# Two-stage kernel (sparse attention, then spectral mixing): uneven weight pieces, a joint mix of last rows, overwritten matmul passes, and separate tiles for z and y

## The chip, the core and the metric

The kernel runs on one NeuronCore of a Trainium2 chip. The metric is the device time of the whole kernel in microseconds (us). The core has a matrix engine (TensorE, "PE" in the profile, with its weight loads "PEld"), a vector engine (VectorE, "DVE"), a scalar engine (ScalarE, "ACT"), GpSimd ("POOL"), a sync engine ("SP") and sixteen transfer engines (DMA). Weights and attention inputs are issued from GpSimd, because these transfers convert from float32 to float16 on the way. Outputs are issued from the sync engine.

## What is computed

The first stage is an attention over 8 batches, 8 heads, 576 tokens and 64 dimensions, with two masks (local for the first four heads, strided for the others). Its result `x` (8 x 576 x 512) goes through the second stage:

```python
X = np.fft.rfft(x, axis=1)
Y = np.zeros_like(X)
Xr, Xi = (np.real(X[:, :n_modes]), np.imag(X[:, :n_modes]))      # n_modes = 64
Yr = np.einsum('bmd,mde->bme', Xr, w_r) - np.einsum('bmd,mde->bme', Xi, w_i)
Yi = np.einsum('bmd,mde->bme', Xr, w_i) + np.einsum('bmd,mde->bme', Xi, w_r)
Y[:, :n_modes] = Yr + 1j * Yi
y = np.fft.irfft(Y, n=S, axis=1)
u = x + y
return (u + np.maximum(u @ w_ch, 0.0)).astype(np.float32)
```

The weights `w_r` and `w_i` hold 64 x 512 x 512 float32 numbers each, so the two together are 134 MB to be read; everything else is small beside them.

## The kernel before

The kernel splits the 512 input columns of each mode into two halves and so has 128 "half modes". They are loaded two at a time into one tile: 64 partitions for the real part, 64 for the imaginary part.

```python
ORDER = [(1, m) for m in range(SPLIT1)] + [(0, m) for m in range(SPLIT0)]
ORDER += [(1, m) for m in range(SPLIT1, NM)] + [(0, m) for m in range(SPLIT0, NM)]
# in w_fetch, for the pair that starts at place i of ORDER:
for ri, src in enumerate((moe_w_r, moe_w_i)):
    dst = wt[ds(64 * ri, 64)]
    ...                                   # rows: the same 64 rows of the source
    ones = range(2)
    if ri and not m:
        ones = [1]
    elif i < 2 * NM - 4:
        nc.gpsimd.dma_start(dst, rows)    # both modes of the pair in one transfer
        continue
    for j in ones:                        # the last four half modes: one transfer for each
        nc.gpsimd.dma_start(dst[:, j], rows[:, j])
```

Each half mode is multiplied in `mode` (16 passes of 128x128 against 16 columns, line 555). While these stream, the kernel turns `x` (`turn`), multiplies it by `w_ch` (`premix`, kept as `v0`, and `x` itself as `xo`), and, as soon as 16 modes are complete, computes their spectra `zz` (multiplied by `w_ch`) and `yy`:

```python
def spec_out(g, b, yp, zp):
    src, dst = ds(32 * (b % 4), 32), ds(32 * g, 32)
    act_copy(zzs[b][dst], zp[src])                              # ScalarE
    nc.vector.tensor_copy(out=yys[b][dst], in_=yp[src])         # VectorE, line 688

def spec_pair(g, bq):                     # the third group, g = 2
    up = psum("u", pair=True)
    zp, yp = up[:, 0], up[:, 1]
    spec_mm(g, bq, yp, zp)
    for b in range(4 * bq, 4 * bq + 4):
        spec_out(g, b, yp, zp)
```

Then `renew` adds the first 48 modes' share to `v0` and `xo`, two row groups at a time, or the last 64 rows of two batches together. One `renew` follows each of the last modes:

```python
def renew(b, ts):
    n = len(ts)
    ...
    vp, up = psum("v", pair=True), psum("u", pair=True)
    for j, t in enumerate(ts):
        nc.tensor.matmul(vp[:, j], idn, v0[:, j], start=True, stop=False)       # line 889
        rows_of(b, t, vp[:, j], zzs, False)                                     # line 696
    act_copy(v0, vp[:, 0:n])
    for j, t in enumerate(ts):
        rows_of(b, t, up[:, j], yys, True)
    nc.vector.tensor_tensor(out=xo, in0=up[:, 0:n], in1=xo, op=AluOp.add)       # line 894

rest = [(0, m) for m in range(SPLIT1, NM)] + [(1, m) for m in range(SPLIT0, NM)]   # 24 modes
NL = len(rest) - 2
for i, (slot, m) in enumerate(rest):
    mode(slot, m)
    upto = min(len(late), -(-len(late) * i // (NL - 1)))
    for w in late[n:upto]:                # 2 spec_pair, then 20 renew
        w()
    n = upto
    if i == NL - 1:
        v_early(0); u_early(0)            # lines 921 and 930: v0 and xo into the accumulators
    elif i == NL:
        u_early(1)
```

After the last mode the tail begins: the last 16 modes' `zp` and `yp` (lines 672 and 679), then for each output item its own rows (`v_early`, `u_early`), the new rows (line 941), a relu on ScalarE (line 955), a sum on VectorE (line 963) and the output transfer (line 971). An item is 128 rows of two batches, 512 KB of output; the last 64 rows of two batches make one of 256 KB.

The last 64 rows of each batch lie in the same tile `xT` as the others before, and `premix` handles them batch by batch with 64 output rows:

```python
xT, cols = xTs[b], out_cols(t)
if t < 4:
    pr = ds(0, 128)
    ...
else:
    pr = ds(64 * (b % 2), 64)
    v0, xo = v0h[b // 2], xoh[b // 2]
for ch in range(4):
    nc.tensor.matmul(vp[pr, :], xT[:, ch, cols], w_chs["cp"][:, ch, :], start=(ch == 0), stop=(ch == 3))
for ch in range(4):
    nc.tensor.transpose(tp[pr, ds(128 * ch, 128)], xT[:, ch, cols], idn)
```

Of the kernel before, what the change touches and what calls it, by code (L numbers as in the profile page):

```python
# [56 lines left out]
def kernel(  # L57
# [91 lines left out]
    ORDER = [(1, m) for m in range(SPLIT1)] + [(0, m) for m in range(SPLIT0)]  # L149
    ORDER += [(1, m) for m in range(SPLIT1, NM)] + [(0, m) for m in range(SPLIT0, NM)]  # L150
    w_tiles = []
    w_chs = {}
    w_ch = big.tile([128, 4, DM], F16, name="w_ch")

    def w_fetch(n=1):
        for _ in range(n):
            i = len(w_tiles)
            if i >= 2 * NM:
                return
            half, m = ORDER[i]  # L160
            if i // 2 in GUEST:
                wt = big.tile([128, 2, 4, DM], F16, tag=GUEST[i // 2], name="wt")
            else:
                wt = pw.tile([128, 2, 4, DM], F16, tag="w", name="wt")
            for ri, src in enumerate((moe_w_r, moe_w_i)):
                dst = wt[ds(64 * ri, 64)]
                rows = src[m : m + 2, ds(256 * half, 256), :].rearrange(
                    "m (p c) e -> p m (c e)", c=4
                )
                dst = dst.rearrange("p m c e -> p m (c e)")  # L170

                ones = range(2)
                if ri and not m:
                    ones = [1]
                elif i < 2 * NM - 4:
                    nc.gpsimd.dma_start(dst, rows)  # L177
                    continue
                for j in ones:
                    nc.gpsimd.dma_start(dst[:, j], rows[:, j])  # L180
            w_tiles.extend((wt[:, 0], wt[:, 1]))
# [405 lines left out]

    xTs = {}

    def turn(b, half, cp):  # L590
        if (half, cp) == (1, 0):
            xTs[b] = ptr.tile([128, 4, S], F16, tag="xT", bufs=2, name="xT")
        xT = xTs[b]
        tp = psum("tp", half=True)
        if half:
            for rp in range(2):
                for j, (a, z) in enumerate(JG):
# [13 lines left out]
            nc.vector.tensor_copy(  # L611
                out=xT[:, 2 + cp, 512:576].rearrange(
                    "p (c r2 rp) -> p rp c r2", r2=16, rp=2
# [14 lines left out]
        )  # L628
        nc.vector.tensor_copy(out=xT[:, cp, 512:S], in_=tp[:, 512:S])

# [8 lines left out]
    def premix(b, t):  # L639
        if t == 0:  # L640
            v0s[b] = px.tile([128, 4, DM], F16, tag="xb", name="v0")
            xos[b] = ptr.tile([128, 4, DM], F16, tag="xo", bufs=8, name="xo")
        xT, cols = xTs[b], out_cols(t)
        if t < 4:
            pr = ds(0, 128)
            v0, xo = v0s[b][:, t, :], xos[b][:, t, :]
        else:
            pr = ds(64 * (b % 2), 64)
            v0, xo = v0h[b // 2], xoh[b // 2]
        vp = psum("sc")  # L650
        tp = psum("tp", half=True)
        for ch in range(4):
            nc.tensor.matmul(  # L653
                vp[pr, :],
                xT[:, ch, cols],
                w_chs["cp"][:, ch, :],
                start=(ch == 0),
                stop=(ch == 3),
            )
        for ch in range(4):  # L660
            nc.tensor.transpose(tp[pr, ds(128 * ch, 128)], xT[:, ch, cols], idn)  # L661
        nc.scalar.activation(out=v0[pr], in_=vp[pr, :], func=ACTF.Copy)  # L662
        nc.vector.tensor_copy(  # L663
            out=xo[pr].rearrange("p (h q c) -> p h q c", h=2, c=4),
            in_=tp[pr, 0:512].rearrange("p (h c q) -> p h q c", h=2, c=4),
        )
# [159 lines left out]
    for b in range(B + 1):  # L826
        for t in range(5):
            if b > 0:
                work.append(lambda b=b, t=t: premix(b - 1, t))
            if b < B and t < 4:  # L830
                half, cp = ((1, 0), (1, 1), (0, 0), (0, 1))[t]
                work.append(lambda b=b, half=half, cp=cp: turn(b, half, cp))
# [40 lines left out]

    def spec_pair(g, bq):
        up = psum("u", pair=True)
        zp, yp = up[:, 0], up[:, 1]
        spec_mm(g, bq, yp, zp)
        for b in range(4 * bq, 4 * bq + 4):
            spec_out(g, b, yp, zp)

    def renew(b, ts):
# [3 lines left out]
        else:  # L885
            v0, xo = v0h[b // 2].unsqueeze(1), xoh[b // 2].unsqueeze(1)
        vp, up = psum("v", pair=True), psum("u", pair=True)
        for j, t in enumerate(ts):
            nc.tensor.matmul(vp[:, j], idn, v0[:, j], start=True, stop=False)
            rows_of(b, t, vp[:, j], zzs, False)  # L890
# [4 lines left out]

    late = [lambda bq=bq: spec_pair(2, bq) for bq in range(2)]
    for b in range(B):
# [28 lines left out]

    def u_early(k):
        ups[k] = psum("u", pair=True)
        for j, r in enumerate(own(items[k], xos, xoh)):
            nc.tensor.matmul(ups[k][:, j], idn, r, start=True, stop=False)  # L930

# [49 lines left out]
    for i, (slot, m) in enumerate(rest):  # L981
        mode(slot, m)
        upto = min(len(late), -(-len(late) * i // (NL - 1)))
        for w in late[n:upto]:
# [5 lines left out]
        elif i == NL:  # L990
            u_early(1)
    yctx.close()
# [70 lines left out]
```

The softmax here doesn't subtract the row's maximum and nothing guards it: scores larger than these inputs give would overflow.

## Time and profile before

| what | value |
|---|---|
| time, median of 3 runs | 431.6 us (431.23 to 432.73) |
| span of the profiled execution | 433.9 us |
| PE busy, PEld busy | 352.9 us, 242.5 us |
| DVE, ACT, POOL busy | 238.9, 206.2, 107.4 us |
| read from memory, written | 162.83 MB, 9.44 MB |
| weight transfers of 512 KB (as written) | 62 + 60, median 18.0 and 19.4 us from issue to landing |
| output transfers of 512 KB | 15, median 3.1 us from issue to landing |
| end of the last output issue | about 429.9 us |

The span is drawn in forty slices of about 10.8 us; a digit is a busy share in tenths, and the row PEclk is the TensorE clock that was granted, in tenths of full speed. The DMA row is the mean busy share of the sixteen transfer engines. A busy PE is not PE at its peak: the same instruction takes longer at a reduced clock. Shares of transfer time can exceed 1 in a stretch, because the records of successive packets overlap a little. The page's chain is the sequence of work that ended last, followed back from the end; its shares say on what the end waited.

### The profile page before, as it was taken

The numbers are of one execution on the slowest core, as the hardware profiler recorded it, in microseconds if no ns is written. First come the engines' busy times: TensorE is split into PE (matmuls) and PEld (weight loads), VectorE is DVE, ScalarE is ACT, GpSimd is POOL, SyncE is SP. The second block draws the span as 40 slices with busy tenths as digits, with TensorE's granted clock in tenths as the row PEclk, the third lists the DMA queues.
The fourth block names the chain that finished last, engine by engine and source line by source line (L and its number), as shares of the span: only waits on it lengthen the run. The fifth ranks groups of instructions, "written<-read, shape, count | busy, mean of one in ns | idle before, by whom it ended". The sixth has DMA issues, their size and how long they took to land.

```text
span 433.9 us, 12303 instructions
## 1 busy us (share of the span) xinstructions
PE 352.9 (81%) x5431; PEld 242.5 (56%) x5431; DVE 238.9 (55%) x465; ACT 206.2 (48%) x361; POOL 107.4 (25%) x191
## 2 busy tenths in 40 slices
PE   2977988789898798987387598986989669998994
PEld 2765777658776576766254365554655425542331
DVE  3888778835444434542114347844784446553595
ACT  1776678644556345565141224421433344443573
POOL 7333332322332122222222222222232213200000
PEclk9999889957899768899555869998999959997798
DMA  8999999999999999999999999999999999981598
GB/s 153 211 210 214 213 213 210 211 211 212 214 212 215 213 213 214 214 214 212 213 213 214 213 214 213 213 214 215 213 213 213 214 213 215 213 177 46 189 350 305
DMA packets 30484, 91.78 MB, mean 212 GB/s; under 512 B 4000, under 2 KB 4768, under 8 KB 30432
## 3 DMA queue, kind: packets, MB, share of 16 engines
q0 software_dynamic: 24704, 81.28, 94.6%
q1 hardware_dynamic: 5216, 9.52, 6.2%
q8 instruction: 42, 0.69, 0.6%
q10 hardware_dynamic: 512, 0.21, 0.2%
q14 instruction: 10, 0.08, 0.0%
HBM read 162.83 MB, written 9.44 MB: 397 GB/s over the span
## 4 chain that ended last, share of the span: by engine, by line
DMA 55%; PE 29%; DVE 8%; ACT 3%; issue 3%; POOL 1%; DVEq 0%; ACTq 0%; POOLq 0%
DMA wt<-in_moe_w_i_dram 41%; DMA wt<-in_moe_w_r_dram 7%; PE y L555 4%; DMA ring<-in_q_dram 3%; PE v L921 3%; DVE yy L688 2%; PE tp L403 2%; PE u L930 2%; PE v L941 2%; DMA ring<-in_k_dram 2%; DVE xb L231 2%; PE sc L522 2%; PE sc L449 2%; PE y L522 2%; PE sc L465 1%
## 5 line engine op out<-in xcount | busy, mean ns | idle before, releaser
L555 PE MATMUL y<-X,wt 128*128 128x16 f16 (+1 forms) x2048 | 81.8, 192 | 31.6 <-DMA wt<-in_moe_w_i_dram 30.4
L555 PEld LDWEIGHTS <-wt 128*128 128x128 f16 (+1 forms) x2048 | 72.0, 101 | 45.6 <-issue 37.0
L177 POOL DMA_DIRECT2D wt<-in_moe_w_r_dram x62 | 36.4, 588 | 169.7 <-PE y L555 93.9
L177 POOL DMA_DIRECT2D wt<-in_moe_w_i_dram x60 | 35.4, 590 | 49.0 <-DMA wt<-in_moe_w_i_dram 37.9
L653 PE MATMUL sc<-w_cp,xT 128*128 128x512 f16 (+1 forms) x160 | 46.0, 414 | 0.0
L662 ACT ACTIVATE v<-sc 128x512 f16<-128x512 f32 x32 | 19.1, 597 | 54.6 <-PE sc L653 54.5
L479 ACT ACTIVATE PL<-sc 128x480 f16<-128x480 f32 (+1 forms) x48 | 27.4, 579 | 33.2 <-PE sc L465 33.0
L663 DVE COPY xo<-tp 128x512 f16<-128x512 f16 x32 | 22.1, 690 | 30.1 <-PE tp L661 30.0
L231 DVE TENSOR_TENSOR xb<-av,rec 90x256 f16<-90x256 f32 (+2 forms) x80 | 36.0, 450 | 2.8
L230 DVE RECIPROCAL rec<-av 90x4 f32<-90x4 f32 (+2 forms) x80 | 14.6, 183 | 36.3 <-PE av L494 25.5
L410 DVE COPY qT<-tp 128x576 f16<-128x576 f16 x16 | 12.0, 758 | 34.4 <-PE tp L403 31.0
L894 DVE TENSOR_TENSOR xo<-u,xo 128x1024 f16<-128x1024 f32 x16 | 19.6, 1224 | 15.9 <-PE u L696 15.8
L241 ACT ACTIVATE v<-tp 128x640 f16<-128x640 f16 (+1 forms) x24 | 19.4, 808 | 17.4 <-PE tp L437 14.8
L403 PE MATMUL tp<-cI_s,ring 64*64 64x64 f16 x864 | 25.3, 206 | 2.8 <-issue 2.0
L963 DVE TENSOR_TENSOR osb<-u,rl 128x1024 f32<-128x1024 f32 (+1 forms) x21 | 22.2, 1071 | 8.9 <-PE u L941 6.1
L368 ACT ACTIVATE PL<-sc 90x360 f16<-90x360 f32 (+1 forms) x48 | 22.8, 490 | 7.6 <-PE sc L361 7.1
L241 ACT ACTIVATE v<-v 128x1024 f16<-128x1024 f32 x16 | 16.4, 1024 | 18.0 <-PE v L696 18.0
L403 PEld LDWEIGHTS <-ring 64*64 64x64 f16 x864 | 19.8, 119 | 7.8 <-issue 4.3
L955 ACT ACTIVATE rl<-v 128x1024 f32<-128x1024 f32 (+1 forms) x21 | 18.8, 901 | 10.3 <-PE u L941 5.0
L449 PE MATMUL sc<-cMl_s,cI_s 128*128 128x480 f16 (+1 forms) x48 | 21.5, 448 | 2.5 <-ACT X L241 1.6
L266 PE MATMUL tp<-cI_s,ring 72*128 72x72 f16 x256 | 15.3, 207 | 8.6 <-DMA ring<-in_v_dram 7.0
L522 PEld LDWEIGHTS <-xb 108*128 108x128 f16 (+2 forms) x176 | 15.6, 108 | 11.7 <-DVE xb L231 7.1
(128 smaller groups left out, 705.3 us busy)
## 6 DMA issues: line engine op xcount, KB each, us to landing
wt<-in_moe_w_r_dram POOLq DMA_DIRECT2D x62, 512.0 KB, 18.0
wt<-in_moe_w_i_dram POOLq DMA_DIRECT2D x60, 512.0 KB, 19.4
out_dram<-osb SPq DMA_DIRECT2D x15, 512.0 KB, 3.1
ring<-in_v_dram POOLq DMA_DIRECT2D x8, 288.0 KB, 13.4
ring<-in_q_dram POOLq DMA_DIRECT2D x8, 288.0 KB, 13.6
ring<-in_k_dram POOLq DMA_DIRECT2D x8, 288.0 KB, 13.0
ring<-in_v_dram POOLq DMA_DIRECT2D x3, 512.0 KB, 14.6
ring<-in_q_dram POOLq DMA_DIRECT2D x3, 512.0 KB, 14.6
```

Of the source, the lines that this page charges most:

```text
L177: nc.gpsimd.dma_start(dst, rows)
L231: nc.vector.tensor_tensor(out=dst, in0=val.rearrange("p h (q c) -> p h c q", c=4), in1=rec[0:n, 0:pieces] .to_broadcast((n, pieces, 64)) . ...
L241: nc.scalar.activation(out=out, in_=in_, func=ACTF.Copy)
L368: nc.scalar.activation(out=PS[0:n, ds(POFF[t], 4 * n)], in_=scp[0:n, 0 : 4 * n], func=ACTF.Exp, scale=SCALE,)
L403: nc.tensor.transpose(tp[ds(64 * hp, 64), ds(64 * i, 64)], qn[ds(64 * hp, 64), ds(64 * (9 * g + i), 64)], idn[ds(64 * hp, 64), ds(64 * hp, ...
L449: nc.tensor.matmul(scp[:, 0 : n * times].rearrange("p (h x) -> p h x", h=times), idn, mask_rows("cMl", n, times), start=True, stop=False,)
L479: nc.scalar.activation(out=dst, in_=src, func=ACTF.Exp, scale=SCALE)
L522: nc.tensor.matmul(xp[:, ds(192 * cp, 192)].rearrange("p (f m) -> p f m", f=3), xb[b][0:n, base + t, ds(128 * cp, 128)], F[0:n, :, t, :], ...
L555: nc.tensor.matmul(yv[:, mi, e, :], wt[pr, XC[c], ds(128 * e, 128)], Xh[half][pr, c, :, :, m], start=(c == 0), stop=(c == 3),)
L653: nc.tensor.matmul(vp[pr, :], xT[:, ch, cols], w_chs["cp"][:, ch, :], start=(ch == 0), stop=(ch == 3),)
L663: nc.vector.tensor_copy(out=xo[pr].rearrange("p (h q c) -> p h q c", h=2, c=4), in_=tp[pr, 0:512].rearrange("p (h c q) -> p h q c", h=2, c=4),
L963: nc.vector.tensor_tensor(out=osb[:, j], in0=up[:, j], in1=rl[:, j], op=AluOp.add)
```

## The change

It has five parts, all of which leave the computed values as they are, apart from the order of independent work.

1. The real parts of three tiles (those that start at places 44, 74 and 102 of the order) are loaded in three pieces of unequal numbers of rows instead of in one transfer of 64 rows. It is for the sharing of the load among the transfer engines.
2. In the last two tiles, which are loaded mode by mode, the transfers are ordered by mode first: real and imaginary part of one mode, then of the other.
3. The last 64 rows of two neighbouring batches are put side by side in one tile `x4`, and mixed together with 128 output rows, once for two batches.
4. The third group's z results for all eight batches share one accumulator tile, and the y results another, so that ScalarE and VectorE each read a tile of their own. The first of the two now comes after the first of the last 24 modes.
5. TensorE is given passes whose result the next pass overwrites (`fill`, and a `u_early` that writes the same rows three times). They are for the clock of TensorE[...].

```diff
+    UNEVEN = {44: (35, 18, 11), 74: (5, 33, 26), 102: (18, 35, 11)}
...
+                elif i in UNEVEN and not ri:
+                    a = 0
+                    for n in UNEVEN[i]:
+                        nc.gpsimd.dma_start(dst[a : a + n], rows[a : a + n])
+                        a += n
+                    continue
                 elif i < 2 * NM - 4:
                     nc.gpsimd.dma_start(dst, rows)
                     continue
-                for j in ones:
-                    nc.gpsimd.dma_start(dst[:, j], rows[:, j])
+                single += [(j, ri, dst[:, j], rows[:, j]) for j in ones]
+            for _, _, to, rows in sorted(single, key=lambda x: x[:2]):
+                nc.gpsimd.dma_start(to, rows)
...
+            if b % 2 == 0:
+                x4s[b // 2] = ptr.tile([128, 4, 128], F16, tag="x4", bufs=2, name="x4")
+        x4 = x4s[b // 2][:, :, ds(64 * (b % 2), 64)]
...
-        nc.vector.tensor_copy(out=xT[:, cp, 512:S], in_=tp[:, 512:S])
+        nc.vector.tensor_copy(out=x4[:, cp], in_=tp[:, 512:S])
...
         else:
-            pr = ds(64 * (b % 2), 64)
+            xT = x4s[b // 2]
             v0, xo = v0h[b // 2], xoh[b // 2]
...
-            if b > 0:
+            if b > 0 and (t < 4 or b % 2 == 0):
                 work.append(lambda b=b, t=t: premix(b - 1, t))
...
-    def spec_pair(g, bq):
+    def spec_late(mm, kept, eng):
         up = psum("u", pair=True)
-        zp, yp = up[:, 0], up[:, 1]
-        spec_mm(g, bq, yp, zp)
-        for b in range(4 * bq, 4 * bq + 4):
-            spec_out(g, b, yp, zp)
+        for bq in range(2):
+            mm(2, bq, up[:, bq])
+        for b in range(B):
+            eng(kept[b][64:96], up[ds(32 * (b % 4), 32), b // 4])
+
+    def fill(acc, n):
+        for _ in range(n):
+            nc.tensor.matmul(acc, idn, v0s[0][:, 0], start=True, stop=True)
...
         vp, up = psum("v", pair=True), psum("u", pair=True)
+        if n == 1:
+            fill(vp[:, 0], 3)
...
-    late = [lambda bq=bq: spec_pair(2, bq) for bq in range(2)]
+    def spec_last():
+        spec_late(spec_y, yys, lambda o, i: nc.vector.tensor_copy(out=o, in_=i))
+        fill(psum("v", pair=True)[:, 0], 5)
+
+    late = [lambda: spec_late(spec_z, zzs, act_copy), spec_last]
...
-    def u_early(k):
+    def u_early(k, times=1):
         ups[k] = psum("u", pair=True)
-        for j, r in enumerate(own(items[k], xos, xoh)):
-            nc.tensor.matmul(ups[k][:, j], idn, r, start=True, stop=False)
+        rows = list(enumerate(own(items[k], xos, xoh)))
+        for n, (j, r) in enumerate(rows * times):
+            nc.tensor.matmul(
+                ups[k][:, j], idn, r, start=True, stop=n < len(rows) * (times - 1)
+            )
...
-        upto = min(len(late), -(-len(late) * i // (NL - 1)))
+        upto = min(len(late), i + 1)
...
-            u_early(1)
+            u_early(1, times=3)
```

## The prediction

> **What bounds the kernel now.** I read the page's forty slices first, then the chain that ended last, and then cut the end of the span into stretches.
>
> ```profile
> PEclk9999889957899768899555869998999959997798
> DMA  8999999999999999999999999999999999981598
> ...
> DMA wt<-in_moe_w_i_dram 41%; DMA wt<-in_moe_w_r_dram 7%; PE y L555 4%; DMA ring<-in_q_dram 3%; PE v L921 3%; DVE yy L688 2%; PE tp L403 2%; PE u L930 2%; PE v L941 2%; DMA ring<-in_k_dram 2%; DVE xb L231 2%; PE sc L522 2%; PE sc L449 2%; PE y L522 2%; PE sc L465 1%
> ```
>
> The transfer engines are full from the second slice to the thirty-fifth, and weights are 48% of the chain. Up to about 390 us nothing that only frees TensorE, ScalarE or VectorE can move the end. After that the clock row shows 7s: part of the final stage runs at a reduced TensorE clock. The same end in stretches (busy us and counts of PE, PEld, DVE, ACT, POOL; granted clock, DMA share, GB/s):
>
> ```profile
> 384.00:387.00 3.00, 2.80 (x31) 1.50 (x28) 1.69 (x2) 1.02 (x1) 0.13 (x1) 1.00 1.02 197
> 387.00:389.00 2.00, 1.80 (x23) 1.09 (x22) 1.22 (x1) 1.02 (x1) 0.00 (x0) 1.00 0.60 121
> 389.00:392.00 3.00, 2.38 (x27) 1.01 (x25) 2.27 (x3) 1.62 (x2) 0.00 (x0) 1.00 0.54 107
> 392.00:394.50 2.50, 1.89 (x23) 0.84 (x22) 0.04 (x1) 0.00 (x0) 0.00 (x0) 1.00 0.07 13
> ```
>
> The share drops to half at 387 and stays there for five us: half of the sixteen engines have nothing left, half do. The trace's completion marks of the last weight transfer agree: eight lie at 387.1 to 389.1 (mean 387.7), seven at 392.3 to 392.9, one at 394.35. Among transfers landing near 100 us the spread of the marks is 3.6 us, near 240 us 5.9, near 350 us 7.0: the lag grows in steps of about 1 us.
>
> ```profile
> 393.25 0.64 PE L555 MATMUL y<-X,wt 128*128 128x16 f16 x16 [0.44 <-DMA wt<-in_moe_w_i_dram]
> 393.72 0.59 PE L930 MATMUL u<-xo,cI_s 128*128 128x512 f16 x2
> 394.48 0.64 PE L555 MATMUL y<-X,wt 128*128 128x16 f16 x16 [0.17 <-DMA wt<-in_moe_w_i_dram]
> 395.51 1.45 PE L672 MATMUL zp<-w_ch,YT 128*128 128x512 f16 x4 [0.39 <-DVE YT L583]
> ```
>
> The last two modes wait for exactly those late marks. Then comes a tail of 38.8 us (395.13 to 433.9). In it TensorE is on the chain nearly throughout, and its pace changes midway:
>
> ```profile
> 398.77 0.96 PE v L921 x2
> ...
> 410.19 0.54 PE v L921 x2
> ```
>
> The same two 512-column passes cost 0.96 us at first and 0.54 later. The clock is 0.50 from 396.0 to 406.2 and full afterwards. At full clock a whole output item (512 KB) takes 1.30 us (eight VectorE sums in 10.38 us), and the output transfers then just keep up (share 1.0, about 378 GB/s, 1.39 us an item).
>
> Last, the mixing of the third spectra group, before the late updates:
>
> ```profile
> DVE yy L688 <- ACT zz L241: 6.6, 7, 2.6
> ACT zz L241 <- DVE yy L688: 4.6, 6, 0.9
> ```
>
> ScalarE and VectorE copy in turn, each waiting for the other; both sets are done only at 351.7, and TensorE idles some 4 us and goes to half clock (348.2 to 358.5).
>
> **What the Trainium skill says.** *TensorE: Matmul & The Clock Gate*, "Part 1: The HAM clock gate": activity in free-running windows of about 3.4 us decides between half and full clock. [...] *DMA: Bandwidth & Descriptors*, "Why a DMA increments its semaphore by 16 and not by 1": a transfer uses the largest number of engines up to 16 that divides its row count, and for software descriptors with fewer than 16 the engines are consecutive from a round-robin cursor. The trace names no engine, so it cannot confirm that. *Runtime: NRT & Kernel Launch*, "Instruction fetch mechanics": instructions come in 16 KiB blocks of 256. Here TensorE's 10,862 instructions make 42.4 such blocks, and the page has 42 packets in queue 8, 0.69 MB, at 0.95 us each: 40 us, which on eight engines is the 5 us by which one half lags. That it is these eight is my inference. *PSUM — Partial Sum Buffer*, "PSUM bank collisions raise a hardware error": two engines in the same bank and quadrant must be kept apart. The z and y results already lie in different banks of one tile, so the observed alternation is an ordering by tile, and separate tiles should end it.
>
> **Part 1, uneven pieces.** By the divisor rule 35 rows go to 7 engines (5 each), 18 to 9 (2), 11 to 11 (1), 5 to 5 (1), 33 to 11 (3), 26 to 13 (2). Earlier only the twelve 8-row loads moved the cursor, 96 places, a multiple of 16, so it is where it started; call that engine 0. Adding the three tiles up, engine 0 gets 14 rows, 1 and 2 get 17, 3 to 6 get 16, 7 gets 13, 8 to 10 get 9, 11 to 15 get 8; even loading gives 12. A row is two 4 KB packets; one 512 KB transfer gives each engine eight and lands every 2.46 us, so 0.31 us a packet. The first eight gain 3.6 rows on average, the others lose 3.6: their gap closes by 7.25 x 2 x 0.31 = 4.5 us, against a gap of 5.1 in the marks. That even the light engine finishing at 389.1 (engine 7's share is only +1) fits makes me believe that the pieces were cut for this profile. The new ends: 389.7 to 390.7 for most, and 394.35 - 2.5 = 391.9 for the straggler. A perfectly even end would be 387 + (0.60x2 + 0.54x3 + 0.07x2.5)/1.06 = 389.8. The last tile thus lands at about 391 to 391.9, 2.5 to 3.4 us sooner. Six more issues of about 0.6 us on GpSimd (107 of 434 us busy) are hidden.
>
> **Part 2, order of the last single transfers.** The real and imaginary halves of one mode now travel together, so the second-last mode is complete after the second of the last four transfers, not the third: 1.2 us sooner. It unblocks TensorE but not the last mode.
>
> **Part 3, joint last rows.** Four of eight groups of 4 passes and 4 transposes (about 0.9 + 0.3 us), 4 ScalarE copies of 0.59 and 4 VectorE copies of 0.69 go away: 5, 2.4 and 2.8 us, at 300 to 340 us beside full transfers. Directly worth nothing; it lets TensorE follow weights that now land 3 us sooner.
>
> **Part 4, z and y apart, and overwritten passes.** Eight ScalarE copies (4.7 us) beside eight VectorE copies (5.5 us) instead of 10 us in turn: late updates begin some 5 us earlier, and five extra passes fill the gap. Before, TensorE ran 2.14 us a mode from 358 on, catching up with weights arriving every 2.46 us, and had caught up by 383; so this too is mostly hidden. The three passes in each update of a last row cost 0.65 us each. Near the end they cost something. From the mode at 389.84 to the end of the early accumulations at 392.8 is 3.0 us; with three passes 3.6; then a mode 0.65 and six passes of 0.22 instead of two, 1.3. That mode's data carried marks at 387.9 and, on the straggler, 389.7; less 2.5, TensorE can start on it at 386 to 387.2 and reaches the last mode at 391.6 to 392.8. That is about where the straggler lets it go: the last mode starts at about 392.0 instead of 394.48, a gain of **2.5 us**.
>
> **The tail at full clock.** The extra passes put about 5,600 columns into the last window before the last mode, well over 3,072. If the clock stays up: four z passes take 0.87 + 0.17 instead of 1.46, the first new rows 0.39 instead of 0.61, together 0.6 to the first relu. Then nineteen pass times up to 406.4 at 0.43 us, 8.2 us, become about 4.7, limited partly by the 1.3 us cadence of ScalarE and VectorE: 3.5 gained. Before ran at full clock from 406.2 on and its output was saturated only from 415, so the rest of the tail simply shifts. The output, 9.44 MB at 378 GB/s = 25 us from its first transfer, would finish about 2.5 us before TensorE's own limit. Tail: **4.1 us**.
>
> Sum: 2.5 + 4.1 = 6.6 us if everything works, 425.0.
>
> **Rivals.** *The clock still falls.* The last mode has only 256 columns in 0.65 us, then a wait of about 0.4 for VectorE and, after 2,560 columns for z and y, another 0.3; a 3.4 us window laid badly over that holds some 3,000 to 3,600, near where it fell before. For: the windows are free-running, and windows of 3,400 to 3,900 went either way. Against: the passes just before are dense. Then only 2.5 us are gained, 429. I give it 30%, with half measures in between. *The pieces go to the wrong engines.* If shares are dealt from another start, the marks spread to over 10 us; the weights end near 397 and the tail's gain is eaten up: 430 to 432. 10%. *TensorE or the output takes over.* The added passes delay the last mode (twenty-one extra, 4.5 us at 0.215, but only seven near the end), or the output at 1.39 us an item binds sooner because TensorE fills it earlier; that caps the gain at about 4 to 5 us: 427.
>
> **Range and chances.** Full success near 425, partial failure 427 to 429, both weighted: 425.4. Over 2% would need 8.6 us, that is the straggler gone as well (landing at 390.5, TensorE ready for it) together with a fully warm tail: 0.13. Slower by over 2% needs both a wrong deal and something unforeseen: 0.02.
>
> **What would show it.** Right: DMA share near 1 up to about 389 and a fall within 2 us; landing marks of the last tile within 3 us; last mode at 391 to 392.5; clock 1.00 from there to 425; the z passes near 0.9 us; tail near 34.7 us; alternate waits of yy and zz gone and no 0.5 clock at 348. Wrong: a half share for several us before the last landing; a last mode released by PE with weights long there; 0.5 in the clock after it; VectorE sums waiting on output buffers.

## The result, and the profile after

The changed kernel takes 434.03 us (median of 4 runs, 433.67 to 434.5) against 431.42 for the kernel before on the same chip: a ratio of 1.0055, interval 1.0032 to 1.0077. It is 2.6 us slower. The prediction was 425.4: it had a gain of some 6 us where there is a loss.

The page of the changed kernel, rows of the forty slices and the chain that ended last:

```profile
PEclk9997999968968869969655578999898989899997
DMA  8999999999999999999999999999999999991698
...
DMA 59%; PE 21%; DVE 9%; ACT 5%; issue 4%; POOL 1%; DVEq 0%; POOLq 0%; ACTq 0%
```

The transfers stay full a little longer than before (the thirty-sixth digit is 9, not 8), and transfers are 59% of the chain. The clock row ends in 89899997: the tail runs at full clock, as was predicted. The same end in stretches (length; busy us and counts of PE, PEld, DVE, ACT, POOL; granted clock, DMA share, GB/s):

```profile
384.00:387.00 3.00, 2.08 (x24) 1.09 (x23) 1.23 (x1) 1.14 (x2) 0.51 (x1) 1.00 1.04 197
387.00:389.00 2.00, 1.80 (x23) 1.03 (x21) 1.23 (x1) 0.91 (x1) 0.00 (x0) 1.00 0.92 180
389.00:392.00 3.00, 2.80 (x40) 1.77 (x39) 1.63 (x2) 1.86 (x2) 0.00 (x0) 1.00 0.46 93
392.00:394.50 2.50, 1.82 (x11) 0.62 (x9) 1.93 (x3) 0.79 (x2) 0.00 (x0) 1.00 0.13 26
```

The half share that lasted from 387 to 392 is gone: 0.92 up to 389, then 0.46 and 0.13 (two of sixteen engines are 0.125). So the load was in fact spread differently, but two engines still run on. The sixteen completion marks of the last weight transfer say it directly (computed from the trace, in us; first line a second profile of the kernel before, which comes below):

```
before, again  386.85 386.92 387.08 387.43 387.45 387.50 388.37 388.56 392.27 392.50 392.53 392.54 392.59 392.61 392.70 393.74
after          388.80 388.82 389.03 389.05 389.29 390.44 390.55 390.74 391.00 391.06 391.15 391.17 391.20 391.24 394.92 395.08
```

Fourteen engines end within 2.4 us, between 388.8 and 391.2; two end at 395. TensorE near the end of the changed kernel, in order of time (start, us, line, operation; in brackets the idle time and what ended it):

```profile
385.33 0.64 PE L564 MATMUL y<-X,wt 128*128 128x16 f16 x16 [0.93 <-DMA wt<-in_moe_w_i_dram]
...
392.24 0.81 PE L894 MATMUL v<-v,cI_s 128*128 128x512 f16 x3 [0.20 <-ACT v L250]
...
395.15 0.64 PE L564 MATMUL y<-X,wt 128*128 128x16 f16 x16
395.62 1.46 PE L952 MATMUL u<-xo,cI_s 128*128 128x512 f16 x6
396.92 0.64 PE L564 MATMUL y<-X,wt 128*128 128x16 f16 x16
397.94 1.04 PE L683 MATMUL zp<-w_ch,YT 128*128 128x512 f16 x4 [0.39 <-DVE YT L592]
```

The mode at 385.33 is the last that waits for weights. From there TensorE has 11.6 us of its own work to the last mode, at 396.92, although the weights of that one landed at 395.08. The chain of waits confirms it: from 385.33 on it holds no transfer until the output.

```profile
385.33 0.64 PE y L564 x16
386.88 1.03 ACT v L250
389.02 1.03 ACT v L250
391.17 1.03 ACT v L250
392.24 0.81 PE v L894 x3
393.64 0.61 ACT v0h L250
```

So the last mode starts at 396.92 instead of the predicted 392.0. The rest of the span, from the end of that mode (397.56) to 432.3, is 34.8 us; predicted was 34.7.

### The profile page after: what moved, and what is told of

Read it like the earlier page. It is cut to its first block, busy times and chain, and to the rows that moved or that the text cites. A ratio compares the mean times of both kernels' runs of the same rounds, so it can differ in the third digit from the quotient of the medians.

```text
span 432.3 us, 12283 instructions
## 1 busy us (share of the span) xinstructions
PE 348.7 (81%) x5420; PEld 240.0 (56%) x5420; DVE 236.3 (55%) x461; ACT 203.5 (47%) x357; POOL 111.0 (26%) x197
## 4 chain that ended last, share of the span: by engine, by line
DMA 59%; PE 21%; DVE 9%; ACT 5%; issue 4%; POOL 1%; DVEq 0%; POOLq 0%; ACTq 0%
DMA wt<-in_moe_w_i_dram 46%; DMA wt<-in_moe_w_r_dram 11%; DVE kz L282 3%; PE y L564 2%; DVE xb L240 2%; PE v L942 2%; PE u L952 2%; PE sc L531 2%; ACT X L250 2%; PE v L965 1%; DMA ring<-in_q_dram 1%; PE tp L412 1%; ACT v L250 1%; DVE rec L239 1%; ACT PL L377 1%
## 5 line engine op out<-in xcount | busy, mean ns | idle before, releaser
L564 PE MATMUL y<-X,wt 128*128 128x16 f16 (+1 forms) x2048 | 82.4, 192 | 37.1 <-DMA wt<-in_moe_w_i_dram 35.3
L564 PEld LDWEIGHTS <-wt 128*128 128x128 f16 (+1 forms) x2048 | 72.9, 102 | 52.0 <-issue 45.3
L185 POOL DMA_DIRECT2D wt<-in_moe_w_r_dram x59 | 34.6, 586 | 128.2 <-PE y L564 50.9
L185 POOL DMA_DIRECT2D wt<-in_moe_w_i_dram x60 | 35.3, 588 | 66.9 <-DMA wt<-in_moe_w_i_dram 47.6
L664 PE MATMUL sc<-w_cp,xT 128*128 128x512 f16 x128 | 40.0, 440 | 1.3 <-DVE xT L637 1.3
L419 DVE COPY qT<-tp 128x576 f16<-128x576 f16 x16 | 12.0, 758 | 39.1 <-PE tp L412 36.2
```

Of the source, the lines that this page charges most:

```text
L564: nc.tensor.matmul(yv[:, mi, e, :], wt[pr, XC[c], ds(128 * e, 128)], Xh[half][pr, c, :, :, m], start=(c == 0), stop=(c == 3),)
L664: nc.tensor.matmul(vp, xT[:, ch], w_chs["cp"][:, ch, :], start=(ch == 0), stop=(ch == 3),)
```

## The experiments

The theory after the result had two parts: the pieces of the weights cost instead of gaining, and the profile of before that the prediction read was not typical. The rivals: the overwritten passes cost, or the new order does.

**The kernel before, profiled again.** No edit.

> The kernel before, profiled a second time. Theory A (the first profile of it was not typical: 435.8 us in that execution against a median of 431.4): the span is about 429.6 us, and the stretch of half clock after the last mode is shorter or missing, so the tail is about 35 us instead of 38.8. Rival B (the profile is typical and only profiling itself costs 4 us): again a span near 434 and half clock for about 10 us after the last mode.

431.65 us, ratio 0.998 (0.9943 to 1.0016). The page's clock row and TensorE's last waits:

```profile
PEclk9999899969899688799855779998999968999998
```

```profile
392.64 0.64 PE L555 MATMUL y<-X,wt 128*128 128x16 f16 x16 [0.39 <-DMA wt<-in_moe_w_i_dram]
393.12 0.59 PE L930 MATMUL u<-xo,cI_s 128*128 128x512 f16 x2
393.87 0.64 PE L555 MATMUL y<-X,wt 128*128 128x16 f16 x16 [0.16 <-DMA wt<-in_moe_w_i_dram]
394.89 1.04 PE L672 MATMUL zp<-w_ch,YT 128*128 128x512 f16 x4 [0.39 <-DVE YT L583]
```

The row ends in 68999998 where the first profile had 59797798. The z passes take 1.04 us, not 1.45, and the tail from the end of the last mode is 34.7 us (394.51 to 429.2), not 38.8. The profile that the prediction read came from an execution of 435.82 us, and this one from 431.06. (Of 281 timed executions of the kernel before, 263 lie between 430.2 and 433.2 us and 18 between 435.0 and 436.3, with none in between; the first profile was of the second kind.) Whatever of the change aims at the clock of the tail could gain nothing in the median.

The number of columns that TensorE streams does not tell the two profiles apart.

**After, with even pieces.**

```diff
-    UNEVEN = {44: (35, 18, 11), 74: (5, 33, 26), 102: (18, 35, 11)}
+    UNEVEN = {}
```

> The changed kernel with the three pieced tiles loaded in one transfer each. Theory A (the pieces fall on the wrong engines: two engines that already lag get 16 rows instead of 12): about 2 us faster than the changed kernel, 432.0 us, and the completion marks of late transfers spread by about 7 us instead of 8.8. Rival B (the pieces are harmless, the cost is in the added passes before the last mode): 434.0 us, no change.

432.21 us, ratio to before 1.0018 (0.9994 to 1.0041). Without the pieces 1.8 of the 2.6 us are gone.

**Before, with the pieces alone.** The edit is the first part of the change, on the kernel before.

> The kernel before with nothing but the three uneven tiles added. Theory A: the lagging engines lag more, 433 to 434 us against 431.4. Rival B: 431.4. Rival C (the pieces do balance the engines here, as the prediction had it): 428.5.

433.47 us, 1.0043 (1.0026 to 1.006): 1.9 us slower. Added or removed, the pieces cost the same.

**After without any overwritten pass; with and without pieces.** `fill` returns at once, and `u_early(1)` writes once.

> The changed kernel without any of the overwritten passes. If they only cost: TensorE reaches the last mode 1.5 us sooner, 432.5 us. If they keep the clock up: the clock falls to half after the last mode and the time is 436 to 438 us. In the first case the clock stays at full in the tail.

434.67 us, 1.006 (1.0039 to 1.0081). In its profile half clock lies at 373.9 to 380.8 and not after the last mode.

> The changed kernel without the uneven pieces and without any overwritten pass: what is left is the joint mix, z and y apart, and the order of the last transfers. Theory A (the overwritten passes cost TensorE 1.4 us before the last mode and win nothing, since the kernel before mostly kept its clock in the tail): 431.0 us, last mode within 0.3 us of its last weight. Rival B (without the passes the clock falls more often): the middle of the runs at 435 us or more, with half clock after the last mode. Rival C (the other parts cost too): 432.2 us as with the passes.

432.27 us, 1.0029 (1.0002 to 1.0056), with four of twelve executions between 435.9 and 439.4; with the passes one of twelve was above 435. In its profile the clock was at half between 384.7 and 391.6. Taken away as a whole, the passes change the median by 0.1 to 0.6 us in the other direction. So as a whole they are not the cost, and the expected gain of 1.4 to 1.5 us did not come. They had to be divided, and this is done further below.

**Which engines get a piece.** First, five tiles with pieces of a single row, which should show which engine each goes to:

```diff
+    UNEVEN = {i: (1, 1, 1, 1, 60) for i in (44, 56, 68, 80, 92)}
```

> The kernel before, with five real parts loaded as four single rows and then 60 rows. A single row goes to one transfer engine alone and moves the start by one; the 60 rows leave one engine out. So the completion marks tell, engine after engine in the order of the ring, which of them lag. Theory A (the engines that lag are not eight neighbours; two of them lie inside the stretch that the uneven pieces favour): lagging and leading engines alternate somewhere in the first eight places. Rival B (they are neighbours, and the stretch merely starts in the wrong place): eight leading engines in a row, then eight lagging.

432.6 us in one run. The marks of a full transfer and of the four single rows after it (from the trace):

```
64 rows  178.89 179.01 179.13 179.20 179.21 179.26 179.28 179.50 181.48 181.52 182.03 182.26 182.45 182.52 182.53 183.03
 1 row   179.09 179.19 179.39 179.40 179.41 179.45 179.68 179.73 181.65 181.68 182.23 182.47 182.62 182.71 182.72 183.20
 1 row   179.29 179.36 179.59 179.62 179.63 179.87 179.88 180.27 181.80 181.85 182.44 182.68 182.80 182.89 182.90 183.37
 1 row   179.48 179.53 179.76 179.79 179.86 180.06 180.38 180.73 181.97 182.00 182.65 182.90 182.97 183.06 183.09 183.54
 1 row   179.67 179.72 179.93 179.95 180.09 180.28 180.84 181.05 182.12 182.16 182.85 183.10 183.14 183.23 183.27 183.71
```

It did not name the engines. The four rows should have gone to four engines, one after the other, but only two marks move far, by 1.55 us in all (179.28 and 179.50 to 180.84 and 181.05, in order of place), and the others by 0.6 to 1.0. The premise of the experiment was wrong, as the packets will show. But it showed a cost: marks move by 0.15 to 0.2 us for each single row, also on engines that carry no byte of it. The mean of the marks moves by 0.21 us; the row's own two packets of 0.31 us would be 0.04.

**The dealing closed or mirrored.** If the dealing goes on from where the last piece ended, also into the next execution, pieces whose engine counts add up to a multiple of sixteen should mend it.

```diff
+    UNEVEN = {i: (27, 28, 9) for i in (44, 64, 84, 104)}     # before_closed; also on after: after_closed
+    UNEVEN = {i: (9, 28, 27) for i in (44, 64, 84, 104)}     # before_mirror
+    UNEVEN = {44: ..., 74: ..., 102: ..., 116: (26, 33, 5)}  # after_returned: the change's three tiles and one more
```

> The kernel before with four real parts in pieces of 27, 28 and 9 rows. These take 9, 14 and 9 engines, 32 places in all, so that the start of the dealing comes back to where it was, in each tile and at the end of the program. From start 0 each tile gives engines 0 to 6 five rows, 7 and 8 four, 9 to 15 three. Theory A (the start carries over from one execution to the next; the uneven pieces of the change move it on by 83 places, 3 beyond a multiple of 16, so later executions deal from a wrong start; eight neighbours lead and eight lag): spread of the last marks 2 to 3 us, last weights at about 391 us, 428.5 to 429.5 us. Rival B (the lagging engines are not neighbours, no such dealing can fit): spread 6 us or more and 432 to 434 us.

> The same pieces in the order 9, 28, 27, which turns the dealing round: engines 0 to 6 three rows, 9 to 15 five. Theory A: the lagging half lags 4.3 us more, spread of the last marks 11 to 12 us, last weights near 397, 433.5 to 436 us. Rival B: about the same as the order 27, 28, 9. Should the start not be 0, the two orders change places.

> The changed kernel with one more pieced tile (26, 33, 5 rows at place 116), which moves the start by 29 and so brings the program's sum to 112, a multiple of 16; the change's own three tiles are as they were. Theory A (start carried over): the change's pieces now do what they were for, spread of the last marks about 3 us, 429 to 430.5 us. Rival B (each execution starts the dealing afresh): 434 us, spread near 9 as in the changed kernel.

> The changed kernel with the four tiles of 27, 28 and 9 rows in place of its own three. Theory A: last weights at about 391, but TensorE, with the added passes, reaches the last mode only at about 392.5 to 393; 429 to 430 us. Rival B: 432 to 434 us.

434.49 (1.0053, interval 1.003 to 1.0077), 434.42 (1.0058, 1.0039 to 1.0078), 434.94 (1.0068, 1.0051 to 1.0084) and 435.36 us (1.0084, 1.0061 to 1.0106). Closing the dealing mends nothing: that theory fell. Opposite dealings cost the same in time, though the last marks differ: two engines at 396.9 and 397.9 in the one, six at 395 to 397 in the other. And the cost grows with the number of tiles in pieces: on the kernel before 0, 3, 4 tiles take 431.6, 433.5, 434.5.

**Equal pieces.** That leaves two causes: the extra transfers themselves, or unequal shares. Pieces of 16, 16 and 32 rows go to all sixteen engines alike.

```diff
-    UNEVEN = {44: (35, 18, 11), 74: (5, 33, 26), 102: (18, 35, 11)}
+    UNEVEN = {i: (16, 16, 32) for i in (44, 74, 102)}        # before_16x3; before_16x4: (44, 64, 84, 104)
```

> Before, with the real parts of the same three tiles (44, 74, 102) in pieces of 16, 16 and 32 rows, equal shares for all sixteen engines. Theory A (the extra transfers cost, some 0.3 us each for six of them): about 433.4 us, as with the unequal pieces (433.47); the last weights land 1.5 to 2 us later than in before (393.7), and all sixteen marks move together. Theory B (the unequal dealing costs: the engines that get more end later): within 0.3 us of before, 431.3 to 431.9; last landing and last mode within 0.5 us of before (393.9). A result at 432.2 to 432.8 would say that each has a share.

> Before, with the real parts of tiles 44, 64, 84 and 104 in pieces of 16, 16 and 32 rows: the tiles and the number of transfers of the run with (27, 28, 9), which took 434.49 us, but with equal shares. Theory A (the extra transfers cost): about 434.4 us. Theory B (the unequal dealing costs): 431.3 to 431.9 us.

432.22 (1.0019, 1.0002 to 1.0035) and 432.42 us (1.0021, 1.0012 to 1.0029). Both theories have a share: six extra transfers cost about 0.7 us and eight about 0.9, some 0.12 us each; the unequal shares add 1.2 us with three tiles and 2 us with four. The profile with eight extra transfers fits this: its last marks lie at 388.2 to 390.2 and 393.3 to 395.1, on average 1.4 us later than in the second profile of before, which is eight times the 0.17 us by which a single row moved the marks. The packets show what an unequal piece brings besides. This line of the page, of the run with equal pieces and then of the one with the change's pieces:

```profile
DMA packets 30580, 91.78 MB, mean 212 GB/s; under 512 B 4096, under 2 KB 4864, under 8 KB 30528
```

```profile
DMA packets 30900, 91.78 MB, mean 213 GB/s; under 512 B 4416, under 2 KB 5184, under 8 KB 30848
```

Before had 4000 packets under 512 bytes; six transfers of sixteen engines add 96. The unequal ones add 320 more, of 4 bytes. That is the number of data packets which the engines left out of each piece would have carried (35 rows: nine engines left out, ten packets each; 18: seven by four; 11: five by two; together 128 a tile, twice, and 64 for the third). An engine that gets no rows gets that many tiny packets instead. The same sum gives the counts of the other kernels in pieces to the packet (4384 for 27, 28 and 9 rows; 4272 and 4368 for the aimed pieces below). It also explains the single rows: that run has 4640, which is 4000, 16 for each of 20 extra transfers, 8 for each of five pieces of 60 rows (fifteen engines) and 14 for each single row. So a single row went to two engines, one packet each, and not to one.

**Where the pieces went.** The marks of the first piece of the first tile, 35 rows, in the run with the pieces on the kernel before, and of the transfer before it (from the trace):

```
64 rows  179.12 179.27 179.28 179.29 179.59 179.75 179.99 180.00 181.81 181.98 182.34 182.50 182.86 183.02 183.05 183.44
35 rows  179.44 179.50 179.92 181.97 182.15 182.18 182.30 182.72 183.04 183.08 183.16 183.19 183.23 183.62 185.60 186.26
```

Eight engines led and eight lagged. Five rows are ten packets, 3.1 us. Three leading engines hardly moved (179.4 to 179.9), so five of the eight leading ones got rows. Two marks lie at 185.6 and 186.3, which only lagging engines reach: two lagging ones got rows. Five and two are the seven that the rule of the prediction gives (largest divisor up to 16), but the prediction had all seven among the leading ones. The changed kernel itself shows the same marks (179.43, 179.51, 179.66; and 185.53, 185.97). In the prediction's sum places 3 to 6, where the two lagging ones lie (see below), get 16 rows instead of 12. Four rows are eight packets, 2.5 us, and by about that much the last two marks of the changed kernel lie behind the lagging engines of before (395.0 against 392.5; the six extra transfers would let one expect somewhat more).

From such counts at later pieces I placed the engines: counted from where the dealing starts, 7 and 8 lead, 9 and 10 lag, one of 11 to 15 leads, and the two lagging ones of the first seven seem to lie between 3 and 6. That 0 to 3 all lead was a guess. Pieces aimed by this and nothing else are the test of it.

```diff
+    UNEVEN = {44: (54, 10), 74: (4, 52, 8), 102: (12, 16, 36)}   # before_aimed, light_aimed
+    UNEVEN = {44: (54, 10), 74: (4, 25, 35)}                     # before_aimed2
```

> Before, with the real parts of three tiles in pieces aimed by what the marks have shown: 44: (54, 10), 74: (4, 52, 8), 102: (12, 16, 36). By the dealing rule the places 0 to 3 get four rows more than even loading gives, place 8 three, place 7 one, and all others two fewer. Theory (places 0 to 3, 7 and 8 lead, and the two lagging ones of the first seven are among 4 to 6): the lagging engines end 2 x 0.62 = 1.2 us sooner relative to the rest, the spread of the last marks falls from 6.9 to 4.5 us or less, the last landing comes at 392.5 to 393.3 instead of 393.7 (five extra transfers cost some 0.6 to 0.8 back), and the time is 430.6 to 431.4. Rival (the places are wrong, the rule only fits afterwards): lagging engines get up to four rows more, the spread is 7.5 us or more, and the time is 433 or more.

> Before, with two tiles only: 44: (54, 10), 74: (4, 25, 35). By the dealing rule places 0 to 2 get four rows more than even loading, 7 and 8 three more, places 3 to 6 one fewer, 9 to 15 two fewer. Three extra transfers. Theory: spread of the last marks 5 to 6 us, time 430.8 to 431.6. Rival (wrong places): spread 7.5 us or more, time 432.5 or more.

430.82 (0.9974, 0.9955 to 0.9994) and 430.77 us (0.9975, 0.9961 to 0.999): both faster than the kernel before, by 0.7 us. The first tile of before_aimed, place by place, bears most of the map out (from the trace). Its 54 rows go to places 0 to 8, six each, 3.7 us. Only one leading mark stays behind, at 179.72, so 7 and 8 both lead; two marks go beyond all others, to 184.61 and 186.43, and these are two lagging ones. The next piece, ten rows, gives one row each to places 9 to 15 and 0 to 2. The mark at 179.72 moves by 0.54 us, to 180.26, as it gets a row; the two late ones move by 0.2, to 184.84 and 186.64, as without. So 0 to 2 lead, and the two lagging ones of the first seven are among 3 to 6. The two-tile version shows the same (179.72 to 180.26; 185.50 and 186.44 to 185.71 and 186.64). Place 3 is not shown by itself.

The last marks of the two-tile version:

```
before_aimed2  385.94 386.46 388.47 389.00 389.15 389.28 389.79 390.75 391.47 391.49 391.53 391.59 391.73 392.22 392.26 392.92
```

The lagging engines end about a microsecond sooner (391.5 to 392.9 instead of 392.3 to 393.7). The spread, which was expected at 5 to 6 us, stays at 7.0; by the map, leading engines in places 3 to 6 and 11 to 15 also got fewer rows. The three-tile version missed its spread as well, 6.2 us instead of 4.5 or less, while its last landing at 393.04 and its time came as expected. In both the time followed the last mark and not the spread. TensorE of the two-tile version:

```profile
391.76 0.65 PE L562 MATMUL y<-X,wt 128*128 128x16 f16 x16
392.25 0.59 PE L937 MATMUL u<-xo,cI_s 128*128 128x512 f16 x2
393.06 0.64 PE L562 MATMUL y<-X,wt 128*128 128x16 f16 x16 [0.22 <-DMA wt<-in_moe_w_i_dram]
```

**The overwritten passes, divided.** After with even pieces, and without the seven passes nearest the end:

```diff
-        if n == 1:
+        if n == 1 and b < B - 1:
             fill(vp[:, 0], 3)
...
-            u_early(1, times=3)
+            u_early(1)
```

> After, with even pieces, and without the seven overwritten passes nearest the end (three in the last update of last rows, four in the doubled and tripled early accumulation); the five passes after the y spectra and the three in each of the first three updates of last rows stay. Theory (the chain of TensorE from the first mode that no longer waits for weights to the last mode is 11.6 us in after with even pieces, and seven passes of about 0.2 us each are 1.4 us of it): the last mode starts at 393.7 to 394.2 instead of 395.29, the clock stays full around 385, and the time is about 431.0 (430.5 to 431.6), level with the kernel before or just below it. Rival (the passes keep the clock full through the first microseconds of the tail, and that is worth more than they cost): the clock shows 0.5 after the last mode in the profile or in part of the executions, the tail grows from 35.3 to 38 us or more, and the median is at or above 432.2, with some executions at 435 or more.

431.48 us, 1.0008 (0.9992 to 1.0023). TensorE of after with even pieces, and then of this run:

```profile
390.61 0.81 PE L894 MATMUL v<-v,cI_s 128*128 128x512 f16 x3 [0.20 <-ACT v L250]
...
393.52 0.64 PE L564 MATMUL y<-X,wt 128*128 128x16 f16 x16
394.00 1.46 PE L952 MATMUL u<-xo,cI_s 128*128 128x512 f16 x6
395.29 0.59 PE L564 MATMUL y<-X,wt 128*128 128x16 f16 x16
```

```profile
392.76 0.64 PE L564 MATMUL y<-X,wt 128*128 128x16 f16 x16
393.23 0.59 PE L952 MATMUL u<-xo,cI_s 128*128 128x512 f16 x2
394.24 0.64 PE L564 MATMUL y<-X,wt 128*128 128x16 f16 x16 [0.42 <-DMA wt<-in_moe_w_i_dram]
```

With the passes the last mode starts 1.05 us later than without, and later than its weights, which land at 394.24 and 394.11 in these two profiles. Without them TensorE waits 0.42 us, so it is ready at 393.82, 1.47 us sooner than with them. The medians differ by 0.7 us; held against their own runs of before (1.0018 and 1.0008) their intervals overlap, so the delay is better shown than its price.

The fourteen passes further from the end may be worth something. They are all that this version has over the one without any pass, which took 432.27 us with four of twelve executions above 435; here none of fourteen is. These intervals overlap too.

**The order of the last single transfers, alone.** On the kernel before:

```diff
-                for j in ones:
-                    nc.gpsimd.dma_start(dst[:, j], rows[:, j])
+                single += [(j, ri, dst[:, j], rows[:, j]) for j in ones]
+            for _, _, to, rows in sorted(single, key=lambda x: x[:2]):
+                nc.gpsimd.dma_start(to, rows)
```

> Before, with nothing but the order of the single transfers of the last two tiles changed (real and imaginary part of one mode together). Theory: the second-last mode starts about 1.2 us sooner (392.0 instead of 393.2 in the first profile of before), the last one still waits for the last landing (within 0.5 us of before), and the time is that of before, 431.2 to 431.7. Rival 1 (TensorE's work between the last two modes lies on the path as well): the last mode starts 0.5 to 1 us sooner, time 430.5 to 431.0. Rival 2 (the new order costs): last mode later, time above 432.

432.04 us, 1.0024 (1.0001 to 1.0046).

```profile
393.19 0.64 PE L557 MATMUL y<-X,wt 128*128 128x16 f16 x16
393.67 0.59 PE L932 MATMUL u<-xo,cI_s 128*128 128x512 f16 x2
394.75 0.64 PE L557 MATMUL y<-X,wt 128*128 128x16 f16 x16 [0.49 <-DMA wt<-in_moe_w_i_dram]
```

The second-last mode no longer waits for weights, but TensorE gets to it only when its own work is done, at 393.19, not at 392.0. The last mode still waits, and starts at 394.75 instead of 393.87. By its own signs the second rival came true, though barely: the order brings nothing and may cost. Eight of its 22 executions lie above 433.8 us, of the 35 of before beside them one. Why is not known.

**A version that beats both.** The version without the seven passes, with the three tiles of aimed pieces:

> The run even_light (after with even pieces and without the seven passes nearest the end, 431.48 us), with the three tiles of before_aimed. Theory: the same gain in landing as in before_aimed, last landing 392.7 to 393.5; TensorE's own chain to the last mode (10.2 us from the first mode that no longer waits) lets about half of it through, so the time is 430.6 to 431.4. Rival (wrong places): 433 or more.

430.49 us, 0.9967 (0.9949 to 0.9985). It is 1.0 us faster than the kernel before and 3.5 faster than the changed kernel. Its margin over the aimed pieces on the kernel before (430.8) is within the scatter. Its profile, of an execution of 431.4 us, does not show the earlier landing that was expected: the last weights land at 394.19, not at 392.7 to 393.5. So the time came as expected, but for this version the way to it is not shown.

What most of the profiles have in common is seen when they are put beside each other (us; the last column is the span less the start of the last mode):

| kernel | last weights land | last mode starts | span | from there to the end |
|---|---|---|---|---|
| before, first profile | 394.35 | 394.48 | 433.9 | 39.4 |
| before, again | 393.74 | 393.87 | 429.2 | 35.3 |
| before, pieces alone | 395.72 | 396.04 | 431.4 | 35.4 |
| after | 395.08 | 396.92 | 432.3 | 35.4 |
| after, even pieces | 394.24 | 395.29 | 430.7 | 35.4 |
| the same, without seven passes | 394.11 | 394.24 | 429.6 | 35.3 |
| before, aimed pieces in two tiles | 392.92 | 393.06 | 428.4 | 35.4 |

But for the first profile the tail in these is the same to 0.1 us, with and without the change: their differences arise before the last mode. Six of the twelve other profiles lie within the same 35.3 to 35.5 us, before_closed at 35.54, and five are longer: 35.8 to 35.9 in three (one of them the aimed pieces in three tiles), 36.2 with single rows, 36.7 for after without any overwritten pass.

## Why the prediction was wrong, by its own steps

**The tail at full clock, 4.1 us: right for the wrong baseline.** After has the tail as worked out (34.8 us against 34.7, z passes 1.04 against 0.87 + 0.17, clock 1.00 to 427.7). But before has it too: 34.7 us in its second profile, from an execution like 263 of the 281. The step that failed is the first, reading the tail of 38.8 us as the kernel's: the profiled execution took 435.82 us, outside the three timed runs (431.23 to 432.73). It could have been seen: its span alone, 433.9 us, is longer than their whole time. The sum 431.6 less 6.6 took a saving measured on one execution off the median of others. In the usual execution the 4.1 us were not there to be gained. That every execution of the long kind has this half clock in its tail is not shown: one such profile was taken. The rival of a clock that still falls (30%) did not occur.

**Part 1, 2.5 to 3.4 us sooner: the failed step is "The first eight gain 3.6 rows on average, the others lose 3.6".** The number of engines for each piece held: the Trainium skill's *DMA: Bandwidth & Descriptors*, "Why a DMA increments its semaphore by 16 and not by 1", gives 35 rows to seven engines, and the marks show five and two. What did not hold was that the first seven were all leading ones. That rested on no line of the trace: it was chosen because one sum came out well ("makes me believe that the pieces were cut for this profile"). Fourteen engines did end about where it said (388.8 to 391.2, against 389.7 to 390.7), but the two lagging ones that were given more end at 395.0 instead of 391.9. The rival "the pieces go to the wrong engines" is what happened, given only 10%, and its 430 to 432 was still too good, as it took the tail's gain as sure. The six extra transfers, called hidden, cost 0.7 us: the prediction counted their issue on GpSimd and not what they take on the sixteen transfer engines, which are the bound.

**Part 2, order: right** that the last mode would gain nothing; the 1.2 us sooner for the mode before it did not come, as TensorE's own work held it. Alone the order is 0.5 us slower, with an interval that nearly reaches zero.

**Part 3, joint last rows, and z and y apart: as predicted, and hidden.** In after the waits of y on z are gone; ScalarE and VectorE each wait once, for TensorE:

```profile
ACT zz L250 <- PE u L683: 2.6, 1, 2.6
```

```profile
DVE yy L914 <- PE u L690: 3.1, 1, 3.1
```

The same copies on ScalarE in the second profile of before (first three lines) and in after with even pieces (last line of the next):

```profile
340.94 0.58 ACT L241 ACTIVATE zz<-u 32x512 f16<-32x512 f32 x1 [2.26 <-PE u L679]
342.27 0.59 ACT L241 ACTIVATE zz<-u 32x512 f16<-32x512 f32 x1 [0.75 <-DVE yy L688]
343.61 0.59 ACT L241 ACTIVATE zz<-u 32x512 f16<-32x512 f32 x1 [0.75 <-DVE yy L688]
```

```profile
342.36 4.80 ACT L250 ACTIVATE zz<-u 32x512 f16<-32x512 f32 x8 [2.36 <-PE u L683]
```

4.8 us in one go, where eight copies took until 350.3. The half clock there shrinks from 10.2 us (348.2 to 358.4) to 3.4 (349.2 to 352.6), but it does not vanish; the prediction had no half clock there. All of it lies beside full transfers. The version that keeps these parts, with even pieces and the order but without the seven passes, is at 431.48 against 431.55: together nothing gained or lost. No run has these parts alone; if the order costs its 0.5 us here too, they and the fourteen passes gain as much.

**Part 4, passes near the end: their cost was right, and the failed step is "TensorE can start on it at 386 to 387.2".** Three and four passes of 0.22 us are 1.5 us by its working; the profiles show TensorE ready 1.47 us later, the last mode 1.05, and the medians 0.7, because part was waiting time. The prediction let them be free by having TensorE start that stretch as soon as its weights, then 2.5 us earlier, were there. In after that mode starts at 391.40 although its weights landed at 390.16, and with even pieces at 389.77 (weights 388.52): TensorE was behind with its own work. In after the weights, late on two engines, let TensorE go only at 385.33, three modes ahead of it, and 11.6 us of TensorE's own work follow up to the last mode. Before took 11.0 us for the same stretch, its waits included (382.92 to 393.87).

The 2.6 us thus come to 1.8 for the pieces (434.03 less 432.21), of which about 0.7 for the number of transfers and the rest for their unequal shares, 0.7 for the seven passes (432.21 less 431.48), and nothing for all else together. The runs come from different chips, so the shares are rough.

## What to carry to other kernels

Hold the profiled execution's time against the timed runs before reading a stage from it: a tail that was 4 us longer than usual became most of a predicted gain. Where the transfer engines are the bound, an extra transfer is not free merely because its issue is hidden. Before dealing load unevenly, find out from completion marks which engines lag, with one piece that goes to few of them. Passes that keep TensorE busy belong where it waits for something else, not in the last microseconds before the data that everything waits for.

## What the runs showed of the hardware that was not expected

- A transfer of one row moved the completion marks of all sixteen engines by 0.15 to 0.2 us or more, where its own data's share is 0.04. It used two engines, one packet each, and four such transfers in a row moved the same two marks most.
- A transfer of unequal shares puts 4-byte packets on the engines that it leaves out, as many as each would have had data packets: 320 in the change's three tiles, and the counts of the other kernels agree.
- Leading and lagging engines are not two neighbouring groups in the order of dealing: of the first seven, five led and two lagged (marks of the 35-row piece); of the next two both led (one mark left at 179.72 by the 54-row piece).
- Fewer rows for every lagging engine (by the map, one or two of some 512) was worth 0.7 us net of its three extra transfers. Of the favoured places, 0 to 2, 7 and 8 are shown to lead; 3 is not.

